# Cosformer attention into a SwiGLU block: two q tiles transposed by DMA, the first output products in another order, v loaded in one piece

## The chip, the cores and the metric

The kernel runs on one core of a Trainium2 chip. The metric is device time in microseconds for one execution of the whole program. Before the change it is 323.94 us, the median of 3 runs (323.75 to 324.62).

## What is computed

```python
# attention: q, k, v are [8 batches, 8 heads, 576 positions, 64]
theta = pi / 2 * pos / S
phi(x) = concat(relu(x) * cos(theta), relu(x) * sin(theta))     # 128 features per head
kv  = einsum('bhsf,bhsd->bhfd', phi(k), v)
z   = sum over s of phi(k)
num = einsum('bhsf,bhfd->bhsd', phi(q), kv)
den = einsum('bhsf,bhf->bhs', phi(q), z) + 1e-6
x   = (num / den), heads side by side                           # [4608 tokens, 512]
# feed-forward
xn  = x / sqrt(mean(x * x) + 1e-6) * rms_g
out = (silu(xn @ w_gate) * (xn @ w_val)) @ w_out                # 512 -> 1536 -> 512
```

Inputs and output are float32; the matrix products run in bf16 with float32 sums.

## The kernel before

**Blocks.** The 4608 tokens are worked in nine blocks of 512. Block b (0 to 7) holds 512 tokens of batch b, as four tiles j = 0 to 3 of 128; the last 64 tokens of every batch are gathered in block 8. The order is 0, 1, 2, 3, 4, 5, 6, 8, 7. Each block has 12 steps n (`gval_step`): eight products of 128x512 for one 128-wide slice of w_gate and w_val (four each, L533, into the banks psG and psV), SiLU on ScalarE (L552), the product of the two on VectorE into `hT` (L553). Four output steps j follow (`out_step`, numbered 12 to 15): 12 products `hT` x `wo` (L556), a copy out of the bank (L280, L282) and a store.

**Attention one block ahead.** While block b - 1 and the beginning of block b run, the attention of batch b is made: phi of k and q (L286 on ScalarE, L288 on VectorE, one half of the features each), a cast of v (L282), the sums kv and z on TensorE (`kvz_pe`, L371 or L364, into psA) and their cast to `kvzs` on ScalarE. Then, for each q tile, the transposed phi(q) in `qpT` is multiplied with `kvzs` (`nd_pe`, L426, into psA). VectorE divides (L466, L469, L476), which frees psA, ScalarE squares (L492), GpSimd makes the root (L497), VectorE norms (L504), and the normed tile is transposed into `xnT`, the operand of L533.

**Two ways to transpose.** `q_tr_dma` and `x_tr_dma` issue a DMA that transposes, on SyncE's queue (SP; L323, L517). `q_tr_pe` and `x_tr_pe` let TensorE do it with eight (or four) products with an identity matrix (L340, L523), into a bank that VectorE or ScalarE then copies out (`q_tr_evac`, L343, the copy itself at L280 or L282). From batch 2 on all q tiles go by DMA. For batch 1, whose attention is made during block 0, all four q tiles go over TensorE; of its normed tiles, three go by DMA and the fourth over TensorE.

**The order by hand.** Nothing is reordered: each engine works in the order in which the program issues. `at(blk, n, where, f, ...)` hangs a piece of work on step n of a block; `where` is "pe" (before the step's products), "mid" (half way, output steps only), "pre" (after the products) or "post" (at the end). Block 0 has an output stage of its own, `out_first`: it takes the 48 products of the four tiles into four banks (psG[0], psG[1], psC[0], psC[1]), every 12 of them standing for one of the steps 12 to 15. Before the change it takes rows m = 0 to 7 of `wo` for tile 0, then for tile 1, 2 and 3, and then rows 8 to 11 for each.

In these output steps of block 0 lies the end of batch 1's attention: the list `X1` puts `nd_pe` of tile 0 in the middle of step 12 (product 6), tile 1 at the start of step 13 (product 12), tile 2 in its middle (18), tile 3 at the start of step 14 (24). The transposes of the q tiles by TensorE stand at "pe" of steps 10, 11, 12 and 13.

**Loads.** SyncE loads k, v and q of batches 2 (q only) to 7. `load_kv` for batches above 2 cuts the 576 rows as 112 partitions and a remainder; before the change v of batch 3 and every k come in one piece for the 112 partitions, v of batches 4 to 7 in two pieces of four heads. `raw` is a ring of five buffers for these loads. GpSimd's queue carries the weights, cast to bf16 on the way, the last of them `wo` in three pieces of four rows, and then k (L109) and v of batch 2.

Of the kernel before, what the change touches and what calls it, by code (L numbers as in the profile page):

```python
# [17 lines left out]
def kernel(  # L18
# [12 lines left out]
    B, H, S, D = q.shape  # L31
# [4 lines left out]
    HP = H // 2  # L36
# [5 lines left out]
    NNT = DFF // P  # L42
# [4 lines left out]
    V, A, G = nc.vector, nc.scalar, nc.gpsimd  # L47
# [11 lines left out]
    psV = [ps.tile([P, 512], FP32, name=f"psV{i}") for i in range(2)]  # L59
    psC = [ps.tile([P, 512], FP32, name=f"psC{i}") for i in range(2)]  # L60
# [8 lines left out]
    def kv_rows(src, b, hps):  # L69
        return src[b, 2 * hps[0] : 2 * hps[1], :, :].rearrange(  # L70
            "(hp hh) (s c) d -> (hh s) hp (c d)", hh=2, c=NC
        )

    def wide(b):
        return b > 2
# [4 lines left out]
    def kv_rows5(src, b, r0, r1):  # L80
        part = src[b, :, 0 : NC5 * (KP - 1), :].rearrange(
            "h (p c) d -> p h (c d)", c=NC5
        )[r0 : min(r1, KP - 1)]
        return bass.AP(part.tensor, part.offset, [[NC5 * D, r1 - r0]] + list(part.ap)[1:])
# [12 lines left out]
    def raw_kv(which, b):  # L97
        t = raw_tile(which, b)
        if wide(b):
            return t[:, :].rearrange("p (h e) -> p h e", h=H)  # L100
        return t[:, 0 : HP * NC * D].rearrange("p (hp e) -> p hp e", hp=HP)
# [4 lines left out]
    def load_kv(which, b, hps=(0, HP), eng=nc.sync):  # L106
        src = k if which == "k" else v
        if not wide(b):
            return eng.dma_start(  # L109
                out=raw_kv(which, b)[:, hps[0] : hps[1], :], in_=kv_rows(src, b, hps)  # L110
            )
        last = KP if b < B - 1 else KP - 1
        parts = ((0, H),) if which == "k" or b == 3 else ((0, HP), (HP, H))
        for r0, r1 in ((0, KM), (KM, last)):
            for h0, h1 in parts if r0 == 0 else ((0, H),):
                eng.dma_start(
                    out=raw_kv(which, b)[r0:r1, h0:h1, :],
                    in_=kv_rows5(src, b, r0, r1)[:, h0:h1, :],
                )
        if last < KP:  # L120
            eng.dma_start(
                out=raw_kv(which, b)[last:KP, :, :].rearrange("p h (c d) -> p h c d", d=D),
                in_=src[b, :, S - 1 : S, :].rearrange("h s d -> s h d").unsqueeze(2)
                .to_broadcast([1, H, NC5, D]),
            )
# [92 lines left out]
    for i in range(3):  # L218
        m, e = math.frexp(left)
        part.append(math.ldexp(round(m * 256), e - 8))  # L220
        left -= part[i]
        G.memset(eps_rows[32 * i : 32 * i + 32, :], part[i] / 32)
    load_kv("k", 1, eng=G)
    load_w(wg, moe_w_gate, 8, NNT)

# [329 lines left out]
    def out_mm(j, n, bank, cols=(0, DM)):  # L555
        nc.tensor.matmul(  # L556
            bank[:, 0 : cols[1] - cols[0]], lhsT=hT[:, n, j * P : (j + 1) * P],
            rhs=wo[:, n, cols[0] : cols[1]], start=(n == 0), stop=(n == NNT - 1),
        )

    def out_store(eng, blk, j, bank, cols=(0, DM)):
        osb = four.tile([P, DM], FP32, name="osb", tag="osb")
        w = cols[1] - cols[0]
        copy(eng, osb[:, 0:w], bank[:, 0:w])
        if blk < 8:
            rows = out[blk * S : blk * S + 512, :].rearrange("(p j) m -> p j m", j=4)
            nc.sync.dma_start(out=rows[:, j, cols[0] : cols[1]], in_=osb[:, 0:w])
        else:
            for i in range(2):
                r0 = (2 * j + i) * S + 512  # L570
                nc.sync.dma_start(
                    out=out[r0 : r0 + 64, cols[0] : cols[1]],
                    in_=osb[64 * i : 64 * i + 64, 0:w],
                )
# [102 lines left out]
    x_sq(0, 1)  # L677
    load_q(1, eng=G)
    load_kv("v", 1, eng=G)
    x_norm(0, 0, (0, HALF))  # L680
    x_norm(0, 0, (HALF, DM))
# [51 lines left out]
    def at(blk, n, where, f, *args):  # L733
        slots.setdefault((blk, n), {}).setdefault(where, []).append((f, args))

    def run(blk, n, where):
        for f, args in slots.get((blk, n), {}).get(where, []):
            f(*args)
# [6 lines left out]
    for j in range(4):  # L745
        at(0, (8, 8, 9, 10)[j], "post", q_phi, V, 1, j, 0)
        at(0, 8 + j, "post", q_phi, A, 1, j, 1)
        bank = (psC[0], psC[1], psV[0], psV[1])[j]
        at(0, 10 + j, "pe", q_tr_pe, 1, j, bank)
        at(0, 10 + j, "pre" if j < 2 else "pe", q_tr_evac, V if j < 2 else A, 1, j, bank)  # L750
    at(0, 8, "post", load_kv, "k", 2, (0, HP), G)
    at(0, 9, "post", v_cast, G, 1, (0, 2))
    at(0, 10, "post", v_cast, V, 1, (2, 4))
# [25 lines left out]
    for nb in range(2, B):  # L779
        b = nb - 1  # L780
# [18 lines left out]
        for j in range(4):  # L799
# [4 lines left out]
            m = n + 2 if first and j == 0 else n + 1  # L804
# [3 lines left out]
    for pair in range(4):  # L808
        b = 2 * pair or 3
# [9 lines left out]
    for nb in range(3, B):  # L819
        b = nb - 2  # L820
# [13 lines left out]
    last_blk = 7  # L834


    def out_first():
        banks = (psG[0], psG[1], psC[0], psC[1])
        todo = [(j, m) for j in range(4) for m in range(8)]
        todo += [(j, m) for j in range(4) for m in range(8, NNT)]  # L840
        for i, (j, m) in enumerate(todo):
            if i % 6 == 0:
                run(0, 12 + i // 12, "mid" if i % 12 else "pe")
            out_mm(j, m, banks[j])
            if m == NNT - 1:
                out_store(V if j % 2 else A, 0, j, banks[j])
            if i % 12 == 11:
                run(0, 12 + i // 12, "pre")
                run(0, 12 + i // 12, "post")
# [27 lines left out]
    for n in range(8, NNT):  # L877
        gval_step(0, n)
    out_first()
    for blk in (1, 2, 3, 4, 5, 6, 8, 7):  # L880
        for n in range(NNT):
# [33 lines left out]
```

## Time and profile before

| | |
|---|---|
| time of the profiled execution | 323.94 us |
| its span (first to last instruction) | 322.2 us |
| median of 3 runs | 323.94 us |
| TensorE busy | 317.4 us, 99% of the span |
| VectorE, ScalarE, GpSimd busy | 184.5, 164.9, 40.4 us |
| granted clock of TensorE | full in all 40 slices |
| DMA moved | 53.76 MB, mean 167 GB/s |

The profile has one row per group of instructions, with the line of the kernel (L533), the engine (PE is TensorE, PEld its weight loads, DVE VectorE, ACT ScalarE, POOL GpSimd, SP SyncE), what it writes and reads, how many there were and how long. In a row of the timeline the first two numbers are the start and the length in microseconds from the span's start; what stands in square brackets is how long the engine was idle before and what ended that. "SPq" is the queue of SyncE, whose rows are issues of DMAs, not the transfers themselves.

The page in 40 slices of 8.05 us shows a full TensorE from the second slice on, and DMA engines that are 90% busy or more up to the middle of the span:

```profile
PE   8999999999999999999999999999999999999996
...
DMA  7999999999999999999699969995531500041002
GB/s 227 233 262 272 286 322 154 276 170 205 217 237 211 194 250 186 223 241 189 161 185 213 213 165 197 198 217 160 102 62 34 116 33 0 0 100 33 1 35 98
```

### The profile page before, as it was taken

To read this page: it belongs to the slowest core of one execution; us is meant where nothing else is said; L and a number is where in the kernel's file an instruction comes from. 1 tells how busy PE (TensorE), PEld (TensorE's weight loads), DVE (VectorE), ACT (ScalarE), POOL (GpSimd) and SP (SyncE) were. 2 spreads that over 40 slices of the span, in tenths; PEclk is the share of its full clock that TensorE was granted. 3 is DMA by queue.
4 is the path that set the end of the run, shared out by engine and by line. 5 is a ranking of instruction groups with operands and counts; after the bars stand their busy time and mean duration, and the time that the engine had idled before them with its cause. 6 is when DMAs were issued, how large, how long until landed. Compare 5 with 4: busy or idle time off the path is not lost.

```text
span 322.2 us, 6049 instructions
## 1 busy us (share of the span) xinstructions
PE 317.4 (99%) x2311; PEld 162.4 (50%) x2311; DVE 184.5 (57%) x378; ACT 164.9 (51%) x318; POOL 40.4 (13%) x77
## 2 busy tenths in 40 slices
PE   8999999999999999999999999999999999999996
PEld 3688564544454445444544445444544444444444
DVE  8876858768447773777457644781676034204410
ACT  5666656754584466554744574447543233223321
POOL 9761211002001100011001100100011000000000
PEclk9999999999999999999999999999999999999999
DMA  7999999999999999999699969995531500041002
GB/s 227 233 262 272 286 322 154 276 170 205 217 237 211 194 250 186 223 241 189 161 185 213 213 165 197 198 217 160 102 62 34 116 33 0 0 100 33 1 35 98
DMA packets 80091, 53.76 MB, mean 167 GB/s; under 512 B 52234, under 2 KB 74046, under 8 KB 80062
## 3 DMA queue, kind: packets, MB, share of 16 engines
q1 hardware_dynamic: 73110, 41.25, 62.6%
q0 software_dynamic: 6944, 12.13, 15.6%
q8 instruction: 18, 0.29, 0.4%
q14 instruction: 11, 0.09, 0.1%
q10 hardware_dynamic: 8, 0.00, 0.0%
HBM read 37.83 MB, written 9.44 MB: 147 GB/s over the span
## 4 chain that ended last, share of the span: by engine, by line
PE 93%; DMA 4%; POOL 2%; issue 0%; ACT 0%; SPq 0%; DVE 0%; POOLq 0%
PE psG L533 27%; PE psV L533 27%; PE psC L556 25%; DMA raw<-in_q_dram 3%; PE psV L623 2%; PE psA L426 2%; PE psG L556 2%; PE psG L623 2%; PE psA L364 2%; DMA xnT_tail<-xn 1%; PE psA L371 1%; POOL qp L288 1%; PE psV L340 0%; PE psA L451 0%; POOL vv L208 0%; PE psC L523 0%
## 5 line engine op out<-in xcount | busy, mean ns | idle before, releaser
L553 DVE TENSOR_TENSOR hT<-psV,sg 128x512 bf16<-128x512 f32 x100 | 68.9, 689 | 97.5 <-PE psV L533 65.1
L552 ACT ACTIVATE sg<-psG 128x512 f32<-128x512 f32 x100 | 59.2, 592 | 62.1 <-PE psG L533 60.6
L533 PE MATMUL psV<-xnT,wv 128*128 128x512 bf16 x352 | 90.3, 379 | 0.0
L533 PE MATMUL psG<-xnT,wg 128*128 128x512 bf16 x352 | 90.3, 379 | 0.0
L556 PE MATMUL psC<-wo,hT 128*128 128x512 bf16 (+1 forms) x408 | 88.9, 376 | 0.0
L556 PEld LDWEIGHTS <-hT 128*128 128x128 bf16 x456 | 43.0, 98 | 47.8
L533 PEld LDWEIGHTS <-wv 128*128 128x128 bf16 x400 | 39.1, 98 | 47.2
L533 PEld LDWEIGHTS <-wg 128*128 128x128 bf16 x400 | 36.9, 98 | 40.2 <-issue 0.7
L497 POOL TENSOR_TENSOR rs<-ms,mhalf 128x1 f32<-128x1 f32 x36 | 20.5, 571 | 194.0 <-ACT scr L492 194.0
L280 ACT COPY osb<-psC 128x512 f32<-128x512 f32 x32 | 18.8, 586 | 50.0 <-PE psC L556 50.0
L492 ACT ACTIVATE scr<-xt 128x513 bf16<-128x513 f32 x36 | 22.8, 634 | 25.2 <-DVE xt L476 25.0
L504 DVE SCALAR_TENSOR_TENSOR xn<-xt,rs,gb 128x512 bf16<-128x512 f32 (+1 forms) x37 | 26.9, 730 | 9.9 <-POOL rs L497 9.9
L286 ACT ACTIVATE kp<-raw,tab 128x256 bf16<-128x256 f32 (+2 forms) x51 | 28.8, 607 | 2.3 <-DMA raw<-in_k_dram 2.3
L476 DVE TENSOR_TENSOR xt<-psA,rec 128x512 f32<-128x512 f32 x36 | 24.9, 691 | 1.2
L286 ACT ACTIVATE qp<-raw,tab 128x512 bf16<-128x512 f32 x32 | 22.7, 714 | 3.1 <-DMA raw<-in_q_dram 3.1
L288 DVE TENSOR_SCALAR kp<-raw,tab 128x256 bf16<-128x256 f32 (+2 forms) x53 | 20.3, 430 | 0.3 <-DMA raw<-in_k_dram 0.3
L288 DVE TENSOR_SCALAR qp<-raw,tab 128x512 bf16<-128x512 f32 x31 | 14.7, 478 | 5.1 <-DMA raw<-in_q_dram 5.1
L426 PEld LDWEIGHTS <-qpT 128*128 128x128 bf16 x224 | 10.5, 97 | 6.7 <-issue 0.7
L533 PE MATMUL psG<-xnT_tail,wg 128*128 128x512 bf16 x48 | 12.3, 379 | 0.4 <-DMA xnT_tail<-xn 0.4
L533 PE MATMUL psV<-xnT_tail,wv 128*128 128x512 bf16 x48 | 12.3, 379 | 0.0
L282 DVE CAST vv<-raw 116x1280 bf16<-116x1280 f32 (+1 forms) x13 | 10.7, 823 | 1.3 <-DMA raw<-in_v_dram 1.3
L426 PE MATMUL psA<-kvzs,qpT 128*128 128x65 bf16 x224 | 11.4, 193 | 0.0
(98 smaller groups left out, 177.0 us busy)
## 6 DMA issues: line engine op xcount, KB each, us to landing
out_dram<-osb SPq DMA_DIRECT2D x31, 256.0 KB
raw<-in_q_dram SPq DMA_DIRECT2D x6, 1024.0 KB
raw<-in_k_dram SPq DMA_DIRECT2D x5, 1120.0 KB
raw<-in_v_dram SPq DMA_DIRECT2D x8, 560.0 KB
raw<-in_k_dram POOLq DMA_DIRECT2D x2, 1152.0 KB, 19.4
raw<-in_v_dram POOLq DMA_DIRECT2D x2, 1152.0 KB, 16.0
wg<-in_moe_w_gate_dram POOLq DMA_DIRECT2D x3, 512.0 KB, 14.0
wv<-in_moe_w_val_dram POOLq DMA_DIRECT2D x3, 512.0 KB, 16.2
```

The lines of the kernel that those rows point to most:

```text
L280: A.copy(out=o, in_=i)
L286: A.activation(out=out_ap, in_=in_ap, func=AF.Relu, scale=scale)
L288: eng.tensor_scalar(out=out_ap, in0=in_ap, scalar1=scale, scalar2=0.0, op0=ALU.mult, op1=ALU.max)
L426: nc.tensor.matmul(heads[:, g, hp, :], lhsT=qpT[:, h, j * P : (j + 1) * P], rhs=kvzs[b][:, g, hp * E : (hp + 1) * E], start=True, stop=True,)
L476: V.tensor_tensor(out=xt[:, 0:DM].rearrange("p (hp g d) -> p g hp d", g=2, d=D), in0=heads[:, :, :, 0:D], in1=rec[:, :, :].unsqueeze(3).to ...
L492: A.activation(out=scr[:, :], in_=xt[:, 0 : DM + 1], func=AF.Square, scale=1.0 / math.sqrt(DM), accum_out=ms[:, :],)
L497: G.tensor_tensor(out=rs[:, :], in0=ms[:, :], in1=mhalf[:, :], op=ALU.pow)
L504: V.scalar_tensor_tensor(out=xn_of[(b, j)][:, c], in0=x_of[(b, j)][:, c], scalar=rs_of[(b, j)][:, :], in1=gb[:, c], op0=ALU.mult, op1=ALU. ...
L533: nc.tensor.matmul(bank[:, cols[0] : cols[1]], lhsT=w[:, t, n * P : (n + 1) * P], rhs=x[:, t, cols[0] : cols[1]], start=(t == 0), stop=(t ...
L552: A.activation(out=sg[:, :], in_=g[:, 0:TB], func=AF.Silu)
L553: V.tensor_tensor(out=hT[:, n, :], in0=v[:, 0:TB], in1=sg[:, :], op=ALU.mult)
L556: nc.tensor.matmul(bank[:, 0 : cols[1] - cols[0]], lhsT=hT[:, n, j * P : (j + 1) * P], rhs=wo[:, n, cols[0] : cols[1]], start=(n == 0), st ...
```

## The change

Three edits:

- q tiles 2 and 3 of batch 1 are transposed by a DMA on SyncE's queue at the end of steps 10 and 11 of block 0, in place of eight products each on TensorE at the beginning of steps 12 and 13 and a copy each on ScalarE.
- `out_first` takes rows 0 to 3 of `wo` for all four tiles, then rows 4 to 7, then rows 8 to 11.
- v of batches 4 and 5 is loaded for all eight heads in one DMA (and the remainder of the rows, as before).

```diff
@@ load_kv
         last = KP if b < B - 1 else KP - 1
-        parts = ((0, H),) if which == "k" or b == 3 else ((0, HP), (HP, H))
+        parts = ((0, H),) if which == "k" or b < 6 else ((0, HP), (HP, H))
@@ the work hung on block 0
     for j in range(4):
         at(0, (8, 8, 9, 10)[j], "post", q_phi, V, 1, j, 0)
         at(0, 8 + j, "post", q_phi, A, 1, j, 1)
-        bank = (psC[0], psC[1], psV[0], psV[1])[j]
-        at(0, 10 + j, "pe", q_tr_pe, 1, j, bank)
-        at(0, 10 + j, "pre" if j < 2 else "pe", q_tr_evac, V if j < 2 else A, 1, j, bank)
+        if j < 2:
+            at(0, 10 + j, "pe", q_tr_pe, 1, j, psC[j])
+            at(0, 10 + j, "pre", q_tr_evac, V, 1, j, psC[j])
+        else:
+            at(0, 8 + j, "post", q_tr_dma, 1, j)
@@ out_first
         banks = (psG[0], psG[1], psC[0], psC[1])
-        todo = [(j, m) for j in range(4) for m in range(8)]
-        todo += [(j, m) for j in range(4) for m in range(8, NNT)]
+        todo = [(j, m) for i in range(0, NNT, 4) for j in range(4) for m in range(i, i + 4)]
```

In each engine's order this shows as follows: TensorE loses 16 transposes and 16 weight loads, and the 32 output products of rows 0 to 7 stand in another order; ScalarE loses two copies; SyncE has two more transposing DMAs, directly after its two loads at the start and ahead of the three of xnT, and two loads of v less. VectorE and GpSimd are unchanged.

## Prediction

> **What bounds the kernel now.** I read the page's busy times first, then what TensorE waited for over the whole span, then the chain of waits around the edited place, then the queues that the change touches. Columns of the second view: who waited, for whom, microseconds in total, times, longest.
>
> ```profile
> PE 317.4 (99%) x2311; PEld 162.4 (50%) x2311; DVE 184.5 (57%) x378; ACT 164.9 (51%) x318; POOL 40.4 (13%) x77
> ```
>
> ```profile
> PE psC L578 <- DVE warm L159: 1.2, 1, 1.2
> PE psG L533 <- DMA xnT_tail<-xn: 0.4, 1, 0.4
> ```
>
> TensorE is busy for 317.4 of 322.2 us and waits 1.6 us in all, none of it between its first instruction and 256 us. So whatever is added to or taken from TensorE's order of work in block 0 goes into the end one for one: nothing behind it has a gap to take up a delay. The chain of waits there (start, length, what):
>
> ```profile
> 40.59 0.45 PE psV L340 x8
> 41.03 1.27 PE psA L371 x72
> 42.30 1.40 PE psG L556 x6
> 43.70 0.24 PE psA L426 x8
> 43.94 1.29 PE psG L556 x6
> 45.24 0.45 PE psV L340 x8
> 45.69 0.24 PE psA L426 x8
> 45.93 0.86 PE psG L556 x4
> 46.79 0.43 PE psC L556 x2
> 47.22 0.33 PE psA L426 x8
> 47.55 1.29 PE psC L556 x6
> 48.85 0.40 PE psA L426 x8
> ```
>
> The two L340 rows are the transposes of q tiles 2 and 3 that the change takes away; the four L426 rows are nd of tiles 0 to 3 of batch 1, which read qpT. L556 between them are the output products.
>
> **The change part by part.**
>
> (a) TensorE loses 16 transposes: 0.45 + 0.45 us in the chain. ACT loses two copies of 0.99 to 1.01 us (L280 qpT<-psV); they are worth nothing, since ACT's next work waits for others: the kvzs cast for TensorE's L371, the squares (L492) for DVE's xt. Not all of the 0.90 us comes back. nd of tile 1 overwrites psA, which DVE frees at the end of its product (44.49 + 0.69 = 45.18); tile 2 follows tile 1 at that pace already (DVE's product ends at 47.10, weights of nd 2 are followed by its matmuls at 47.15). So nd 1 can come at about 45.23 less the 0.45 of the first removal, where TensorE would like to be there 0.45 earlier still (45.52 - 0.90 = 44.62 in the same timeline); the wait is 45.23 - 0.45 - 44.62 = 0.16 us. Gain of (a): 0.90 - 0.16 = 0.74 us. Bounds 0.6 to 0.9.
>
> (b) Two transposes by DMA are put at the head of SP's queue, behind the first two loads and ahead of the three of xnT. SP is idle there: its first work after the start is at 47.78. So they are issued when both halves of their phi are written: tile 2 after 38.08 + 0.71 = 38.79, tile 3 after 40.26 + 0.71 = 40.97 (DVE's halves are done at 37.43 and 39.61).
>
> ```profile
> 38.08 0.71 ACT L286 ACTIVATE qp<-raw,tab 128x512 bf16<-128x512 f32 x1
> ...
> 40.26 0.71 ACT L286 ACTIVATE qp<-raw,tab 128x512 bf16<-128x512 f32 x1
> ```
>
> On SP each costs 1.25 us (the L323 rows, 1231/1246/1815 ns), so SP is free at 42.3, 5 us before its next work; the queue it is moved past on SP is not late. They must have landed when TensorE reaches nd 2 and nd 3: 47.22 - 0.74 = 46.5 and 48.85 - 0.74 = 48.1. That leaves 7.7 and 7.1 us. With DMA engines that have nothing else to do this is ample: the trace's packets show the transpose issued at 60.52 (the first L323 of block 1) as 1,024 packets of 256 B between 61.70 and 63.11, that is 1.41 us of all 16 engines and 2.6 us from issue; a reader on TensorE starts 0.5 us after the last packet (xnT_tail: last packet 256.4, matmul 256.9). Alone they would be there at 41.9 and 44.1.
>
> But they are not alone. The queue of POOL holds the last weights and k and v of batch 2:
>
> ```profile
> 24.55 0.74 POOL L184 DMA_DIRECT2D wo<-in_moe_w_out_dram x1 [1.50 <-DMA wv<-in_moe_w_val_dram]
> 27.66 0.76 POOL L109 DMA_DIRECT2D raw<-in_k_dram  x1 [2.37 <-DVE hT L650]
> ...
> 39.15 0.77 POOL L109 DMA_DIRECT2D raw<-in_v_dram  x1
> ```
>
> At 40.0 us, 757 packets of wo (98 ns each) and 512 of k and v (185 ns) are still to go: 10.7 us of work per engine, ending at 51.0 us on the last one. All engines are full until then (window, width, busy of each engine, clock, then DMA share and GB/s at the end):
>
> ```profile
> 40.00:41.00 1.00, 1.00 (x13) 0.66 (x13) 1.00 (x3) 0.97 (x2) 0.00 (x0) 1.00 1.24 205
> 45.00:46.00 1.00, 1.00 (x20) 0.80 (x18) 0.21 (x2) 0.73 (x3) 0.00 (x0) 1.00 1.01 398
> 49.00:50.00 1.00, 1.00 (x13) 0.53 (x11) 0.93 (x4) 0.63 (x2) 0.29 (x1) 1.00 1.61 251
> 51.00:52.00 1.00, 1.00 (x6) 0.48 (x5) 0.16 (x2) 0.45 (x3) 0.55 (x1) 1.00 1.99 146
> ```
>
> What a transpose does beside this traffic, the trace shows in one place only: the xnT transpose issued at 47.78. It has 512 packets of 18 ns, 0.7 us alone. Its first start at 49.05; from 49.3 to 49.7 they run at 44 per 0.1 us, as eight engines would deliver, while eight others still work on v; and it is done only at about 51.4, after the last packet of v (51.01). So it got the engines that had become free and little of the others: 3.6 us from issue with 3.2 us of v in front of it.
>
> The unknown is thus when tile 3 lands. Lower bound: it shares engine time half and half, or is let through: tile 2 takes 2 x 1.41 from 40.0, tile 3 the next 2.8, read from 46.1 on, in time, cost nothing. Upper bound: nothing passes until the loads are through on every engine: 51.0, then 2 x 1.41 and 0.5: 54.3. Packet for packet in turn, tile 2 needs 64 turns of the slowest engine and is through near 48 to 50, but tile 3 still needs what is left of k and v: the last engine's total is fixed, 51.0 + 2 x 64 x 18.5 ns = 53.4, read at 53.9. I take 53.9, since the one row that shows the case ended with the loads and not before. nd 3 then starts at 53.9 instead of 48.85: +5.05 us, and this includes the gain of (a), which is eaten. The 5.66 us from nd 3 to block 1's first matmul (54.51) stay, as their own chain (xt, L492, L497, L504, L523) starts from nd 3.
>
> The Trainium skill, page "DMA: Bandwidth & Descriptors", section "Queues, rings and completion order", says that each engine takes the queues in turn, one whole packet at a time, a packet being some 9 to 17 descriptors and at most 64. The row of 49 us neither confirms nor excludes it. If a tile's share of an engine went as one such packet, tile 3 would be through by about 46 and the sum would be a gain of 0.74 us; if each of the trace's packets is one, it is the forecast's 53.9.
>
> Who is behind the wait: on SP the three xnT transposes and load_q of batch 2, all later than nd 2 by the same 4 us as before, so they move with it; behind TensorE everything. k and v of batch 2 are delayed by the transposes' 2.8 us at most: v lands at 39.15 + 12.4 = 51.5 now, its cast runs at 55.8 and would run 5 us later.
>
> (c) The output products of block 0 in fours: the same 48 matmuls, the last 16 the same. psC is touched from product 8 on, about 44 us; its last reader is done at 41.07. Rows 4 to 7 of wo are now needed at product 16 (about 46.0) and not at product 4 (43.16 before). They landed 22.27 + 20.7 = 43.0, so in the old order TensorE, 0.45 us earlier, would have waited 0.3 us, and up to 3 if the transposes delay wo by 2.8. With the new order: nothing. Rows 8 to 11 (24.55 + 20.9 = 45.5, at most 48.3) are needed at 50.2: nothing.
>
> (d) v of batches 4 and 5 in one piece: two fewer issues on SP of 0.5 us each, at 102.8 and 134.6 us. Same bytes. Their casts come about 35 us later (from 148.6 and 182.4 for the last ones), and TensorE waits for nothing there. Nothing.
>
> Sum of the profiled execution: 323.94 us (span 322.2 and 1.74 around it), which is also the median of the runs. 323.94 + 5.05 = **329.0**.
>
> **The rivals.** R1, the transposes are let through beside the loads: nd 2 and 3 are in time and (a) stands alone: 323.94 - 0.74 = **323.2**, 323.0 to 323.4. For it: 7 us of slack against 1.4 us of work each. Against: the 49 us row. It decides from tile 3 landing before 47.6. R2, the transposes get a turn only between one load and the next: tile 3 goes in after k and before v. Half of the 512 packets are through near 47; 47.0 + 2.8 + 0.5 = 50.3, so +1.45 us: **325.4**. R3, the transposes hold back wo: rows 4 to 7 land up to 2.8 late (45.8) against a need at 46.0; only beyond that TensorE waits, and it would wait for tile 2 anyway; inside the forecast's price. That the change doesn't do what it says can't be: the new issues stand on SP ahead of xnT with nothing to wait for but phi.
>
> **How the numbers follow.** About 0.3%, 0.97 us, is what a measurement can tell from no change. Forecast (stall of tile 3 to the end of the loads) 0.58, its own range 327 to 330.3 (tile 2 held until 52.6 first, and 1.7 us from nd 2 to nd 3, give 54.3 and more); R2 and anything between 0.16; R1 0.26, whose 0.74 us lies just inside the bound: I give 0.14 to same and 0.12 to faster. R2 is slower with 0.15. Slower 0.73, same 0.15, faster 0.12. The range reaches to R1: 323.0 to 330.3.
>
> **What would show it.** TensorE's waits would name L426 and the DMA qpT<-qp, some 6 us in two pieces near 46 and 48 to 54 us; block 1's first L533 on psG would start near 59.6 instead of 54.5; SP's timeline would have two L323 near 38.9 and 41.1; the DMA share would stay near 1 to 53. If no wait at L426 appears and block 1 starts at 53.8, R1 holds. A wait of TensorE at L556 for wo before 46 would mean that I have (c) wrong; a chain that no longer runs over TensorE after block 1 would make all of this wrong.

## The result, and the profile after

The changed kernel takes 334.43 us (median of 6 runs, 333.16 to 334.91) against 324.11 us for the kernel before (6 runs, 323.75 to 324.62): a ratio of 1.0313, 95% interval 1.0293 to 1.0333. The change makes it slower by 10.3 us. The prediction said slower, by 5.05 us, and its range ended at 330.3: the direction holds, and so does the kind of wait, a transpose that is held behind the loads. But TensorE waited for tile 2 and not for tile 3, and the size is half of what came.

The profiled execution took 334.42 us with a span of 332.6. From its page, the busy times, the granted clock in 40 slices of 8.3 us, and TensorE's row for nd:

```profile
PE 317.8 (96%) x2295; PEld 161.8 (49%) x2295; DVE 184.8 (56%) x378; ACT 163.3 (49%) x316; POOL 40.5 (12%) x77
...
PEclk9999995899999999999999999999999999999999
...
L426 PE MATMUL psA<-kvzs,qpT 128*128 128x65 bf16 x224 | 11.7, 195 | 10.4 <-DMA qpT<-qp 10.4
```

TensorE has 16 instructions less and is busy for 0.4 us more; its share fell from 99% to 96%. The whole of the new idle time stands in one place, one wait of 10.4 us for the transposed q. The clock, full in every slice before, is 0.5 and 0.8 of full speed in two slices.

The chain of waits of the changed kernel around that place (start, length, what):

```profile
38.76 18.07 DMA qpT<-qp
56.83 0.04 issue
56.88 0.62 PE psA L426 x8
57.50 2.56 PE psG L556 x6
60.06 0.26 PE psA L426 x8
60.31 1.73 PE psC L556 x8
```

Where TensorE's transposes stood, one DMA is now 18.07 us long. It is tile 2's. nd of tile 2 starts at 56.88 (47.15 before). Six output products then take 2.56 us instead of 1.29, and nd of tile 3 follows without a wait of its own, at 59.85 (48.84 before). Block 1 starts at 65.56 instead of 54.54: 11.0 us late, of which 0.6 come back later, 0.4 of them because block 8 no longer waits for its last transpose.

The windows of the changed kernel (stretch, width, busy time of each engine, clock, DMA share, GB/s):

```profile
44.00:45.00 1.00, 1.00 (x13) 0.49 (x12) 0.68 (x1) 0.23 (x1) 0.00 (x0) 1.00 2.83 124
45.00:46.00 1.00, 1.00 (x10) 0.46 (x7) 0.76 (x3) 0.50 (x2) 0.42 (x1) 1.00 0.06 9
46.00:47.00 1.00, 0.43 (x2) 0.00 (x0) 0.96 (x2) 0.58 (x2) 0.15 (x1) 1.00 0.91 205
49.00:50.00 1.00, 0.00 (x0) 0.00 (x0) 0.00 (x0) 0.00 (x0) 0.00 (x0) 0.86 1.01 366
52.00:53.00 1.00, 0.00 (x0) 0.00 (x0) 0.00 (x0) 0.00 (x0) 0.00 (x0) 0.50 1.37 251
```

Two things are new beside the queueing that was forecast. From 44.6 to 46.2 hardly a packet starts on any DMA engine (9 GB/s from 45 to 46, where the kernel before moved 398). And in the stall the granted clock falls to 0.50.

The packet records of the trace give the rest. They have a queue, a size and two times each, but not the DMA engine; what is said of single engines below is inferred from how many packets are in flight at once. The transposes' first packet starts at 42.65, 3.9 us after the issue; in the run with no traffic below it is 1.3 us. From 48.6 to 51.0, 193 packets of the transposes start and 184 of k and v: as many of one as of the other, as when each engine takes them in turn. The last packet on GpSimd's queue ends at 56.0 (51.0 before), and tile 2 lands 0.8 us later.

### The profile page after: what moved, and what is told of

The parts are those of the page before. It is cut to its first block, busy times and chain, and to the rows that moved or that the text cites. A ratio compares the mean times of both kernels' runs of the same rounds, so it can differ in the third digit from the quotient of the medians.

```text
span 332.6 us, 6014 instructions
## 1 busy us (share of the span) xinstructions
PE 317.8 (96%) x2295; PEld 161.8 (49%) x2295; DVE 184.8 (56%) x378; ACT 163.3 (49%) x316; POOL 40.5 (12%) x77
## 4 chain that ended last, share of the span: by engine, by line
PE 89%; DMA 8%; POOL 2%; issue 0%; ACT 0%; DVE 0%; POOLq 0%
PE psG L533 26%; PE psC L556 26%; PE psV L533 25%; DMA qpT<-qp 5%; DMA raw<-in_q_dram 3%; PE psV L623 2%; PE psA L426 2%; PE psG L623 2%; PE psA L364 2%; PE psG L556 2%; POOL qp L288 1%; PE psA L451 0%; POOL vv L208 0%; PE psC L523 0%; PE psA L371 0%
## 5 line engine op out<-in xcount | busy, mean ns | idle before, releaser
L556 PEld LDWEIGHTS <-hT 128*128 128x128 bf16 x456 | 43.2, 98 | 48.5 <-issue 1.1
L426 PE MATMUL psA<-kvzs,qpT 128*128 128x65 bf16 x224 | 11.7, 195 | 10.4 <-DMA qpT<-qp 10.4
L466 DVE TENSOR_SCALAR rec<-psA 128x8 f32<-128x8 f32 x32 | 5.1, 160 | 14.0 <-PE psA L426 14.0
## 6 DMA issues: line engine op xcount, KB each, us to landing
raw<-in_v_dram POOLq DMA_DIRECT2D x2, 1152.0 KB, 18.5
```

Source lines behind the costliest of these rows:

```text
L426: nc.tensor.matmul(heads[:, g, hp, :], lhsT=qpT[:, h, j * P : (j + 1) * P], rhs=kvzs[b][:, g, hp * E : (hp + 1) * E], start=True, stop=True,)
L556: nc.tensor.matmul(bank[:, 0 : cols[1] - cols[0]], lhsT=hT[:, n, j * P : (j + 1) * P], rhs=wo[:, n, cols[0] : cols[1]], start=(n == 0), st ...
```

## The experiments

Each time is a median beside runs of the kernel before on the same chip (323.6 to 323.9 us).

**The two other edits alone.** The kernel before with

```diff
-        parts = ((0, H),) if which == "k" or b == 3 else ((0, HP), (HP, H))
+        parts = ((0, H),) if which == "k" or b < 6 else ((0, HP), (HP, H))
...
-        todo = [(j, m) for j in range(4) for m in range(8)]
-        todo += [(j, m) for j in range(4) for m in range(8, NNT)]
+        todo = [(j, m) for i in range(0, NNT, 4) for j in range(4) for m in range(i, i + 4)]
```

> The kernel before with two of the three edits: the output products of block 0 in fours and v of batches 4 and 5 in one piece; the four q tiles stay on TensorE. My theory (the DMA transposes alone cost the time): 324.1 us, within 0.3 of the kernel before. Rival (the new order of the products or the larger loads cost part of the 10.3 us): 325 us or more, with a wait of TensorE at L556 or at a later block's L426.

Measured: 323.89 us, ratio 1.0001 (0.9992 to 1.0010). The order of the products and the larger loads cost and bring nothing here.

**The transposes alone.** The kernel before with

```diff
-        bank = (psC[0], psC[1], psV[0], psV[1])[j]
-        at(0, 10 + j, "pe", q_tr_pe, 1, j, bank)
-        at(0, 10 + j, "pre" if j < 2 else "pe", q_tr_evac, V if j < 2 else A, 1, j, bank)
+        if j < 2:
+            at(0, 10 + j, "pe", q_tr_pe, 1, j, psC[j])
+            at(0, 10 + j, "pre", q_tr_evac, V, 1, j, psC[j])
+        else:
+            at(0, 8 + j, "post", q_tr_dma, 1, j)
```

> The kernel before with only q tiles 2 and 3 of batch 1 transposed by DMA. My theory: 334 us, and TensorE waits some 10 us for the DMA qpT<-qp. If the order of the products shields TensorE from wo, as I worked out, wo is now waited for as well, but inside the same stall. Rival (the other two edits carry a part): 331 us or less.

Measured: 334.43 us (332.76 to 336.60), ratio 1.0328 (1.0286 to 1.0370). Together with the run before: the two DMAs carry the whole loss. The profiled execution, the shortest of the four, waits 7.4 us for qpT, where some 10 were expected, and none for wo, which was expected to be waited for; so the new order of the products was not needed as a shield there.

**The stall filled with matmuls.**

```diff
+        if j == 2:
+            at(0, *at_nd, filler, 45, psV[0])
         for f in (nd_pe, nd_post, x_sq):
             at(0, *at_nd, f, 1, j)
```

> The changed kernel with 45 matmuls of zeros on TensorE in the place where it waits for q tile 2 (45 x 0.216 = 9.7 us, from about 46.4 to 56.1; they add work whose result is not used). Theory A (of the stall's price, about 1.3 us is the halved clock after it: 2.56 us instead of 1.29 for six output products): the landing stays near 56.8, the granted clock stays at 1.00, nd 3 follows nd 2 by 1.7 us instead of 3.2, and the time is 333.1 us. Rival B (the products after the stall are slow for another reason): 334.4 us. Rival C (the filler outlasts the landing): 335 us or more.

Measured: 332.46 us, ratio 1.0271 (1.0253 to 1.0289), 1.97 us less than the changed kernel. The chain of waits of this run:

```profile
56.29 0.05 issue
56.34 0.42 PE psA L426 x8
56.75 1.29 PE psG L556 x6
58.05 0.33 PE psA L426 x8
```

The granted clock stays at 1.00; the six products take 1.29 us; nd 3 starts 1.63 us after nd 2 instead of 2.97. That is theory A: 1.3 us of the loss is the halved clock. (The remaining 0.6 us: the landing itself was 0.5 us earlier in this execution, 56.3.) TensorE does 45 matmuls more here and the kernel is faster for it.

**Less traffic beside the transposes.** In the first run k and v of batch 2 are not loaded, in the second only v is not. The edit of the first (the second takes out the line of v alone, and sets `raw` for v alone):

```diff
-    at(0, 8, "post", load_kv, "k", 2, (0, HP), G)
+    raw_tile("k", 1), raw_tile("v", 1)
+    raw[("k", 2)], raw[("v", 2)] = raw[("k", 1)], raw[("v", 1)]
...
-    at(0, 10, "post", load_kv, "v", 2, (0, HP), G)
```

> The changed kernel without the loads of k and v of batch 2 on GpSimd's queue: batch 2 is computed with k and v of batch 1. 757 packets of wo are then the only traffic beside the transposes. Theory A (engines take the two queues packet by packet, and a transpose is done when the slowest engine has had its 64 turns beside what is left on GpSimd's queue): tile 2 lands at 46.5 to 48.5, tile 3 within 1.5 us after it, and the time is 323.5 to 325.5 us. Rival B (a transpose beside any traffic pays a late start and a standstill of some microseconds, whatever is queued): tile 2 lands after 50 and the time is 328 us or more.

> The changed kernel without the load of v of batch 2 (batch 2 uses v of batch 1); k of batch 2 stays. It lies between the changed kernel (256 + 256 packets of k and v left) and the run without both. Theory A (the transposes are done when GpSimd's queue is through on the slowest engine; v is 16 packets per engine, each with one of a transpose beside it, 16 x 0.21 = 3.4 us): tile 2 lands at 52 to 53.5 and the time is 329 to 331.5 us. Rival B (the last load in the queue decides nothing, as tile 2 has had its 64 turns before): it lands after 55, 333 us or more.

Measured: 325.46 us without both (ratio 1.0049, 1.0029 to 1.0069; nd 2 starts at 48.62) and 331.09 us without v (1.0225, 1.0202 to 1.0248; nd 2 at 52.37). Both are theory A: take a load away from GpSimd's queue, and tile 2 lands earlier with the end of that queue. Without v the queue ends 4.6 us earlier and tile 2 lands 4.5 us earlier. Without both it is 9.8 and 8.3 us, and the landing (48.58) is just past what was expected, since 1 us of standstill falls between the queue's end (46.17) and the landing. TensorE's waits there:

```profile
PE psA L426 <- DMA qpT<-qp: 2.0, 1, 2.0
```

**No traffic at all, with its control.** As the run without k and v, and in addition the edit below; once with the DMA transposes, once with all four tiles on TensorE.

```diff
-            rhs=wo[:, n, cols[0] : cols[1]], start=(n == 0), stop=(n == NNT - 1),
+            rhs=wo[:, n % 4, cols[0] : cols[1]], start=(n == 0), stop=(n == NNT - 1),
...
-    load_wo(4, 8)
-    load_wo(8, 12)
```

> The changed kernel with GpSimd's queue emptied ahead of the transposes: k and v of batch 2 are not loaded (batch 2 uses those of batch 1), and of wo only rows 0 to 3, which stand in for rows 4 to 11 too. Theory (only the traffic makes the transposes late): tile 2 lands near 42, tile 3 near 44, TensorE waits for neither, and against the run beside it with the transposes on TensorE the time is 0.74 us less (0.6 to 0.9). Rival (a transposing DMA is late or stands still by itself at this place): TensorE waits for qpT and the time is not less.

> The same loads left out as in the run beside it (k and v of batch 2, rows 4 to 11 of wo), but all four q tiles transposed on TensorE, as before the change. It is the control for the price of the 16 transposes: 323.8 us, as the kernel before, since TensorE waits for none of these loads.

Measured: 322.87 us with the DMAs, ratio 0.9969 (0.9958 to 0.9981), and 324.50 us for the control (1.0022, 1.0006 to 1.0039). The control's times spread from 323.37 to 326.85: its profiled execution starts the first products 3 us late, so the two times can't be subtracted (they differ by 1.63 us, where 0.74 was expected). Why the control is slower than the kernel before, against the expectation, is not shown. The distances can be subtracted. From the first kvz product (L371) to block 1 it is 13.27 us with the DMAs and 13.55 in the control (13.57 in the kernel before); tile 2's transposes, 0.45 us, stood ahead of that. The gain is 0.28 + 0.45 = 0.73 us, and none of it is lost to a wait. The timeline of TensorE in the run with DMAs shows nd 0 to 3 at the pace that was worked out (start, length):

```profile
43.35 0.41 PE L426 MATMUL psA<-kvzs,qpT 128*128 128x65 bf16 x8
...
45.04 0.40 PE L426 MATMUL psA<-kvzs,qpT 128*128 128x65 bf16 x8
...
46.66 0.40 PE L426 MATMUL psA<-kvzs,qpT 128*128 128x65 bf16 x8
...
48.37 0.40 PE L426 MATMUL psA<-kvzs,qpT 128*128 128x65 bf16 x8
```

**One transpose instead of two.** Tile 2 goes back to TensorE, tile 3 stays a DMA.

```diff
-        if j < 2:
-            at(0, 10 + j, "pe", q_tr_pe, 1, j, psC[j])
-            at(0, 10 + j, "pre", q_tr_evac, V, 1, j, psC[j])
+        if j < 3:
+            bank = (psC[0], psC[1], psV[0])[j]
+            at(0, 10 + j, "pe", q_tr_pe, 1, j, bank)
+            at(0, 10 + j, "pre" if j < 2 else "pe", q_tr_evac, V if j < 2 else A, 1, j, bank)
         else:
             at(0, 8 + j, "post", q_tr_dma, 1, j)
```

> The changed kernel with tile 2 back on TensorE: one transpose by DMA instead of two, of tile 3. Theory A (the transpose is done when the slowest engine is through with the loads, whether one or two are in flight; two only add their own packets): it lands at 53 to 55.5, nd 3 waits 5 to 7 us, the clock halves after it, and the time is 329 to 332.5 us. Rival B (it is two transposes in flight that slow each other): it lands before 51 and the time is 327 us or less.

Measured: 330.09 us, ratio 1.0191 (1.0177 to 1.0204); nd 3 starts at 53.05 after a wait of 4.4 us. Theory A by the time, and by the landing at its edge (53.0); the wait is shorter than the 5 to 7 us expected:

```profile
PE psA L426 <- DMA qpT<-qp: 4.4, 1, 4.4
```

But GpSimd's queue ends at 51.92 here, 0.9 us later than before the change, and not 5 us later as with both: about what 64 more packets of 18 ns on each engine take. So theory A's addition, that two only add their own packets (53.4), is too small by some 3 us for the changed kernel (56.00), and there a part of rival B stays. In the execution of the transposes alone it comes out (53.45).

**k and v of batch 2 on the other queue.**

```diff
-    at(0, 8, "post", load_kv, "k", 2, (0, HP), G)
...
-    at(0, 10, "post", load_kv, "v", 2, (0, HP), G)
+    at(0, 11, "post", load_kv, "k", 2)
...
+    at(0, *X1[2][1], load_kv, "v", 2)
     at(0, *X1[3][1], load_q, 2)
```

> The changed kernel with k and v of batch 2 issued on SP's queue: k behind the two transposes of q, v behind the three of xnT and ahead of q of batch 2. Only wo then shares the engines with the transposes. Theory A: nd 2 waits about 2 us as in the run without these loads, nothing later waits, 325 to 326 us. Rival B (the xnT transposes now stand behind k, and q of batch 2 behind v, and TensorE waits there): 327 us or more. Rival C (behind the transposes on one queue the loads do not hold them up, and the standstill does not come): 323.2 us, better than both kernels.

Measured: 327.16 us, ratio 1.0099 (1.0083 to 1.0115). TensorE's waits:

```profile
PE psA L426 <- DMA qpT<-qp: 2.0, 1, 2.0
...
PE psV L533 <- DVE hT L553: 1.0, 1, 1.0
PE psA L371 <- DVE kp L288: 0.8, 1, 0.8
```

A and B each to a part: wo alone costs the same 2.0 us as above, and v, issued at 54.1 only since SP had waited for tile 2's normed transpose, lands at 60.1 and is waited for downstream. C falls. This is 7.3 us better than the changed kernel and 3.3 us worse than the one before.

**TensorE's instruction fetch.** In the changed kernel and the seven runs above that transpose q by DMA, a 16 KB fetch of TensorE's instructions starts 0.3 to 1.7 us ahead of a standstill, long or short.

```diff
-    filler(10, psC[1])
+    filler(2, psC[1])
+    for _ in range(80):
+        nc.tensor.matmul(psC[1][:, 0:8], lhsT=warm[:, 0:P], rhs=warm[:, 0:8], start=True, stop=True)
```

> The changed kernel with 80 small matmuls of zeros (8 columns; nothing uses the result) in place of eight of the ten filler matmuls at the very start. They move TensorE's fetches of instructions (16 KB, 256 instructions each), one of which stands at 44.27 us in the changed kernel, just ahead of 1.6 us in which no DMA engine starts a packet. Theory A (a fetch of TensorE's instructions that meets a transpose in flight stops them both and what is behind them): the fetch comes some 4 us earlier relative to the output products, ahead of the transposes' first packet, no standstill of over 0.5 us is seen before tile 2 lands, and nd 2 comes 1 to 2 us sooner after the first output product. Rival B (the standstill belongs to the meeting of transposes and loads): it stays, at whatever time the fetch comes. The start of the kernel may shift, so it is judged from distances in the trace, not from the time.

Measured: the fetch runs from 43.29 to 44.2, ahead of the transposes' first packet at 45.84, and the standstill is still there, with no fetch in flight and no packet of wo left (from 46.85 to 48.0 only 4 packets of the transposes and 8 of the loads start). The windows of this run:

```profile
46.00:47.00 1.00, 1.00 (x13) 0.64 (x12) 0.23 (x2) 0.00 (x0) 0.00 (x0) 1.00 1.92 302
47.00:48.00 1.00, 1.00 (x8) 0.38 (x6) 0.83 (x2) 0.04 (x1) 0.00 (x0) 1.00 0.13 28
```

Theory A falls. B is not shown by it either: in the run without traffic, only 16 packets start between 43.5 and 44.0 in the midst of tile 3's transpose, with no load left, at the end of a fetch (42.09 to 43.55). What stops the engines stays open. The time, 332.58 us (ratio 1.0258, 1.0229 to 1.0287), is no measure here, since the start is later: the transposes are issued at 41.95 instead of 38.76, and still land sooner, at 54.0.

**Issued nine microseconds later.** That last line asked for a run in which only the issue is late.

```diff
-            at(0, 8 + j, "post", q_tr_dma, 1, j)
+            pass
...
         at(0, *X1[j][1], x_tr_dma, 1, j)
+        if j == 0:
+            at(0, *X1[j][1], q_tr_dma, 1, 2)
+            at(0, *X1[j][1], q_tr_dma, 1, 3)
```

> The changed kernel with the two transposes of q put behind the first transpose of xnT on SP's queue: they are issued at about 48 us instead of 38.8 and 40.9, when wo is through and only k and v of batch 2 are left. Theory A (it is the meeting with the last pieces of wo and the standstill at 44 to 46 us that put off the end of GpSimd's queue from 51.0 to 56.0; the transposes land about 1 us after that end, whenever they were issued): the queue ends at 51.5 to 53.5, nd 2 starts at 52.5 to 55, and the time is 329.5 to 332.5 us, less than the changed kernel's although the transposes start 9 us later. Rival B (the landing follows the issue, 16 to 18 us behind it, or what is issued later lands later): nd 2 starts after 58 and the time is 335 us or more.

Measured: 331.04 us, ratio 1.0221 (1.0202 to 1.0240). The chain of waits:

```profile
48.50 4.51 DMA qpT<-qp
53.01 0.05 issue
53.06 0.62 PE psA L426 x8
```

Theory A: issued at 48.5 instead of 38.76, tile 2 lands at 53.0 instead of 56.8, and the kernel is 3.4 us faster than the changed one. GpSimd's queue ends at 51.10, as in the kernel before (51.01), and no standstill is seen; no fetch of TensorE's instructions meets the transposes in this run either (44.33 to 45.29).

All runs with traffic in one table, by the packet records of each profiled execution:

| kernel | wo packets left at the transposes' first packet | GpSimd's queue ends | nd that waited starts | its time |
|---|---|---|---|---|
| changed | 228 | 56.00 | 56.88 | 334.42 |
| changed, stall filled | 207 | 55.46 | 56.34 | 332.48 |
| transposes alone | 97 | 53.45 | 54.40 | 332.76 |
| late start (fetch moved) | 0 | 52.87 | 54.06 | 332.72 |
| tile 3 only | 0 | 51.92 | 53.05 | 329.90 |
| issued late | 0 | 51.10 | 53.06 | 330.87 |
| without v | 167 | 51.36 | 52.37 | 330.82 |
| k and v on SP | 141 | 46.30 | 48.76 | 327.65 |
| without k and v | 150 | 46.17 | 48.62 | 326.34 |

In every row the waiting nd starts 0.9 to 2.5 us after the end of GpSimd's queue, whether the DMA was issued at 39 or at 48 us. And among the six rows with all loads on GpSimd's queue, that end is the later the more packets of wo the transposes still met, from 51 to 56 us; the three rows with none spread from 51.1 to 52.9.

## Why the prediction was wrong in size and right in kind

The sum's steps, with what they measured:

- Gain of (a), 0.74 us with 0.16 us lost to psA's release: 0.73 us by distances, nd 0 to nd 1 at 1.69 us as worked out. Right.
- Edits (c) and (d) at nothing: ratio 1.0001. Right.
- The stall to the end of the loads: the landing follows the end of GpSimd's queue in every run with traffic. Right as a mechanism, and R1 and R2 fall. But it was forecast for tile 3, and tile 2 was the one waited for.
- **The term that failed first:** "the last engine's total is fixed, 51.0 + 2 x 64 x 18.5 ns = 53.4, read at 53.9". The queue ended at 56.0 and tile 2 landed at 56.83, 2.9 us more. k and v were put off by 5.0 us, not by "2.8 us at most". The total isn't fixed. One transpose did add only about its own packets (51.92), and so did two that came after wo (51.10); but two that met the last pieces of wo put the end off by 4.5 to 5 us in the two executions that met 200 packets or more. The packet records of the changed kernel say where the 5.0 us went: 3.4 ahead of the end of wo's last packet (48.63 against 45.19 before), 1.6 behind it, as k and v took turns with the transposes. In the 3.4 us lies the standstill, about 1.6. The transposes did not make wo's packets longer at first: of the 228 that started after the transposes' first, the 173 up to 44.0 took 97 ns, as before. Six were caught in the standstill at 1.74 us each, and the 32 that followed on those six engines took 183, with k and v behind them. That it was the meeting with wo which brought this about is the reading of the table, not the result of a run that changes wo alone; and the execution of the transposes alone, which met 97, ended as the sum had it, at 53.45.
- **The term that failed next:** tile 2 was set "through near 48 to 50", so that nd 2 would be out of the way when tile 3 landed. It landed at 56.83, and nd 2, six products and nd 3 stood behind it. The prediction let the transposes begin at 40.0, and their first packet started at 42.65. From then on 228 packets of wo and 512 of k and v were to start, 46 for each of the 16 engines on average: taken in turn, that is less than the 64 turns of tile 2 (an estimate from the packet counts). So even an engine with the mean load is not through with tile 2 when its loads end, and the slowest comes last of all: 1,024 packets, as many as tile 2 has, had started by 52.9, 3.9 us before tile 2 landed. The prediction named this case as the upper end of its own range (1.7 us from nd 2 to nd 3).
- "SP is free at 42.3": the second transpose held SP to 53.0 (12.0 us in place of 1.25), and the three of xnT were issued from 53.03 on. No wait of TensorE shows a price for it.
- **The term that was missing:** the clock. Of the 2.97 us from nd 2 to nd 3, 1.3 are the halved clock, by the run that fills the stall.

So the 11.0 us by which nd 3, and with it block 1, starts late are 5.05 forecast, 2.98 by which nd 2 (56.88) starts after the forecast reading at 53.9, and 2.97 from nd 2 to nd 3.

The Trainium skill, page "DMA: Bandwidth & Descriptors", section "Queues, rings and completion order", has the engines take the queues in turn, a whole packet at a time. The changed kernel's records agree, if each of them is taken as a packet: 193 to 184 beside k and v from 48.6 to 51.0 us, so that 256 B wait for 4,608 B, and 156 to 164 of the loads, nearly all wo, from 42.8 to 44.0. What the rule does not account for is the 3.9 us before the transposes' first packet.

The same skill, page "TensorE: Matmul & The Clock Gate", section "What's actually happening", says that the clock halves after an idle window of about 3.4 us and comes back after as long a busy one, and that the window runs free. In the changed kernel TensorE's last product ends near 46.4 and the clock falls at about 49.7 (0.86 in the slice from 49 to 50), and is back at about 60, 3 us after the work. Two other runs differ from that rule as it stands: a wait shorter than the window can be enough, and need not be. A wait of 2.0 us halved the clock in the run without k and v (first line; 0.50 up to 52): the clock fell at 49.2, 0.6 us after the work had begun again, and the six products between nd 2 and nd 3 took 2.41 us there (second line). In the run with k and v on SP, whose profile holds no record of the clock, they took 1.46 us after the same wait, the pace of the full clock (third line, start, length):

```profile
49.00:50.00 1.00, 1.00 (x6) 0.40 (x3) 0.85 (x3) 0.00 (x0) 0.00 (x0) 0.62 0.66 81
...
48.88 2.41 PE L556 MATMUL psG<-wo,hT 128*128 128x512 bf16 x6
...
49.01 1.46 PE L556 MATMUL psG<-wo,hT 128*128 128x512 bf16 x6
```

## What to carry to other kernels

A queue that is idle at its issuer says nothing about the engines behind it: before work is moved from a full TensorE to DMA, look at what the DMA engines still have to do at that moment, on the slowest of them and not on average, and count the packets, since 256 B in turn with 4,608 B waits for the large ones. A small DMA that is needed soon can land earlier when it is issued later, after the large loads. When the one engine that bounds a kernel is made to wait for several microseconds, add the slower clock after the wait to the price; keeping it busy with work that nobody uses took 1.3 us off here.

None of the versions that carry all the loads beats the kernel before. With nothing in the way the two transposes by DMA are worth 0.7 us, so a better order of the loads could bring about 0.2% of the time with them; an order in which wo comes earlier was not tried.

## What was not expected of the hardware

- A standstill of all DMA engines: 3 packets of a transpose and 3 of a load start from 44.6 to 46.2 us in the changed kernel, where the kernel before starts some 140. It is 1.2 us long in the run with the moved fetch, and is absent in the run with the late issue. Its cause is open; neither TensorE's instruction fetch nor a packet of wo is needed for it, as the run with the moved fetch shows.
- In the eight runs in which the wo loads, which are cast on the way, had 2.8 us or more still to go when the transposes were issued, their first packet starts 3.9 to 4.0 us after the issue. In the run with no traffic, where the last packets of wo end 1.0 us after the issue, it is 1.3 us; beside k and v alone it is 1.3 and 1.7 us (xnT's first, in the kernel before issued at 47.78 with its first packet at 49.05, in the run with the late issue 47.09 and 48.82). Waiting behind wo's packets does not explain it: in the run with the moved fetch wo's last packet ended at 44.77 and the transposes' first started at 45.84. The cause is open.
- The issue of the second transpose held SP for 12.0 us in the changed kernel (1.25 with free queues): the issuing queue is blocked along with its DMAs. The row of the issues, shortest, median and longest in ns:

```profile
L323 SPq DMA_TRANSPOSE qpT<-qp x2: 1336/6690/12044, 38.8 to 40.9; - x2
```
